# A new load order, six buffers for transposed weight blocks, one DRAM round trip removed, and zero matmuls ahead of the first rows

## The chip, the cores and the metric

The kernel runs on one core of a Trainium2 chip. The metric is the device time of one execution in microseconds (us): the median of 3 runs of the kernel before is 375.06 us (373.87 to 377.57). TensorE (PE in the profile) multiplies matrices into PSUM, its weight loads are listed apart as PEld, ScalarE is ACT, VectorE is DVE, GpSimd is POOL, SyncE is SP. Transfers are issued by SP or POOL and carried by 16 DMA engines that all queues share.

## The reference

The kernel computes a layer and its gradients. Forward, with x of 2048 rows by 448 columns:

```
n  = layernorm(x)                      # over the 448 columns
h  = x + irfft2(rfft2(n) * (w_r + i w_i))
u  = gelu(einsum("bsd,sf->bdf", layernorm(h), w1) + b1)
out= h + transpose(einsum("bdf,fs->bds", u, w2) + b2)
```

Here w1 is 2048 by 1792 and w2 is 1792 by 2048. Backward, from grad_out: the gradients of x, w_r, w_i, w1, b1, w2 and b2. Everything is bfloat16 at the borders. The Fourier transforms are written as products with tables of cosines and sines.

## The kernel before

**Stages on TensorE.** `fft_rows` (L311) multiplies folded, normalized rows of x by a small table, in four groups g of four row tiles h. `fft_cols` (L321 to L343) does the transform over columns and leaves the spectrum `xs`. `cmul` (L362 to L365, VectorE) multiplies it by the weights `w_t`. `ifft_cols` (L377, L378) and `ifft_rows` (L405 to L414, once for each of 16 row tiles) go back. Between them lies a product that needs nothing of this: `dg(j)` (L434), 14 blocks j of 16 matmuls of 448 columns, w2 transposed times grad_out. Its blocks stand in the program after the Fourier work, and the planner that puts the instructions of each engine in a fixed order sets them into the places where TensorE would wait. After them come `gelu_in` (L515, w1 times the normalized h), the second product of the forward pass (L582, w2), the gradient through w1 (L637, w1 transposed), the backward Fourier stages with `gw2` (L656) between them, and the last gradient (L726). An engine executes its instructions strictly in the planned order: one that waits holds up all that stand behind it.

**The first rows.** For each group g, `Norm.stats` (L279, L281, VectorE) takes mean and variance of four row tiles; `Norm.finish` (L289 to L296) computes the reciprocal deviation and lets ScalarE write the normalized rows `xln`; VectorE folds them into `eo` (L303 to L305); TensorE runs 16 matmuls of 128 columns (L311); the results are cast from PSUM into `zt` by ScalarE or VectorE (L194, L196) as the letters in `"avav"` say (a is ScalarE, v is VectorE). `dg(j)` may not start before `fft_rows` of group min(j-1, 3) has been issued; `dg(0)` is free.

**The load queue.** Nearly all loads stand in one chain on SP: `nxt` ties each one behind the one before it (`tc.issue_after(chain[-1].ins)`), so the order in which the lines are traced is the order in which SP issues them. Up to the last chunk of w1 it is:

```
x0, grad_out 0, x1, grad_out 1, w2T0, x2, x3, w2T1, w2T2, w2T3, w2T4 (after dg 0),
df1, hf, w_r, w_i, w2T5, w2T6, w2T7, hi, di0, kinv, ident, xln_d 0..3 (stores),
w2T8, w2T9, w1c0, w2T10, xs_d (store), w2T11, w1c1, w2T12, w2T13, w1c2, w1c3
```

`w2T` j is a block of w2 loaded with a transposing DMA (L175); it lies in the ring `w4` of four buffers, so that the load j+4 waits until `dg(j)` has read its buffer. The ring is used again for `w1T` (transposed w1, L637), `s6` and `s4` (results on their way out). `w1c` are the chunks of w1 (two DMAs each), `df1`, `hf`, `hi`, `di0`, `kinv`, `ident` are tables. Loads outside the chain (`w1T`, `w2c`) are placed by the planner.

**Two scratch tensors in DRAM** matter here. `xln_d` receives the normalized x after the first stage, by four DMAs on SP, and is read back by four DMAs on POOL into `xr` near the end, where the backward pass of the first layernorm needs it (`norm_back`, L605 to L613). `xs_d` receives the spectrum.

**Biases.** b1 and b2 are turned into columns by two small matmuls with the identity (L503), traced after `dg(13)`, and copied out of PSUM by VectorE (L504).

Of the kernel before, what the change touches and what calls it, by code (L numbers as in the profile page):

```python
# [113 lines left out]
def kernel(  # L114
# [32 lines left out]
    def w4(shape, name):  # L147
        return ring.tile(shape, BF16, tag="w4", bufs=4, name=name)

# [94 lines left out]
    for g in range(2):  # L244
        nxt(ld, go_nat[:, 8 * g:8 * g + 8, :],
            grad_out[0].rearrange("(t p) d -> p t d", p=P)[:, 8 * g:8 * g + 8, :])
        if g == 0:
            load_x(1)
    load_w2T()
    load_x(2)  # L250
    load_x(3)
    for j in range(3):
        load_w2T()

    rstd_x = consts.tile([P, NT], F32, name="rstd_x")
    rstd_h = consts.tile([P, NT], F32, name="rstd_h")
    rneg_x = consts.tile([P, NT], F32, name="rneg_x")
    rneg_h = consts.tile([P, NT], F32, name="rneg_h")
    gb1 = consts.tile([P, NFB], F32, name="gb1")
    gb2 = consts.tile([P, NT], F32, name="gb2")  # L260

    xln_d = dram.tile([P, NT, D], BF16, name="xln_d")
    xs_d = dram.tile([P, 2, XW], BF16, name="xs_d")
# [6 lines left out]
    class Norm:  # L270
        def __init__(self, src, dst, rstd, rneg, eps_col, scale, back, nm):
            self.src, self.dst, self.rstd, self.eps_col, self.scale, self.nm = src, dst, rstd, eps_col, scale, nm
            self.rneg, self.back = rneg, back
# [11 lines left out]
        def finish(self, g):  # L285
            mv = self.mv[:, :].rearrange("p (i c) -> p i c", c=2)
            r = self.rstd[:, 4 * g:4 * g + 4]
            sq = col(4, f"sq_{self.nm}")
            ac.activation(out=sq[:], in_=mv[:, :, 1], func=ACT.Sqrt, bias=self.eps_col[:], scale=self.scale)  # L289
            ve.reciprocal(out=r, in_=sq[:])  # L290
            ve.tensor_scalar(out=self.rneg[:, 4 * g:4 * g + 4], in0=r, scalar1=self.back, scalar2=None, op0=ALU.mult)
            nb = col(4, f"nb_{self.nm}")
            ve.scalar_tensor_tensor(out=nb[:], in0=mv[:, :, 0], scalar=-1.0, in1=r, op0=ALU.mult, op1=ALU.mult)
            for i in range(4):
                h = 4 * g + i
                ac.activation(out=self.dst[:, h, :], in_=self.src[:, h, :], func=ACT.Identity,  # L296
                              scale=self.rstd[:, h:h + 1], bias=nb[:, i:i + 1])

# [71 lines left out]

    def ifft_cols(ys, ab):
        def half(r):
            pt = ps_sp([P, 2, 2, P])
            lo = 1 if r <= 8 else 0
            for c in range(2):
                k = r * DF + 97 * c
                pe.matmul(pt[:, c, :, :], lhsT=ys[:, 0, k:k + P], rhs=hi[:, lo:lo + 2, r, :], start=True, stop=False)  # L377
                pe.matmul(pt[:, c, :, :], lhsT=ys[:, 1, k:k + P], rhs=hi[:, 1 - lo:3 - lo, r, :],  # L378
                          start=False, stop=True)
            return pt  # L380

# [36 lines left out]
    xln = slot(1, [P, NT, D], "xln")  # L418
    nx = Norm(x, xln, rstd_x, rneg_x, eps_x, 1.0, -1.0 / D, "x")
    zt = slot(2, [P, 4, NR, P], "zt")  # L420
    folded = []
    for g in range(4):
        for i in range(4):
            nx.stats(4 * g + i)
        folded.append(fft_rows(xln, zt, g, "avav" if g else "aava"))

# [11 lines left out]
    dg(0)  # L438
    df1 = table([P, 6 * DF], "df1", "df")
    hf = consts.tile([P, 3, NR, P], BF16, name="hf")  # L440
    nxt(ld, hf[:, 0:2], hnd["hf"].ap())
    w_t = slot(4, [P, 2, XW], "w_t")
    load_w(w_t, nxt)
    for j in range(1, 4):
        dg(j)
    hi = consts.tile([P, 3, NR, P], BF16, name="hi")
# [48 lines left out]
    b1col = consts.tile([P, NFB], F32, name="b1col")  # L495
    b2col = consts.tile([P, NT], F32, name="b2col")
    b1r = consts.tile([NFB, P], BF16, name="b1r")
    ld(b1r[:], B_b1.rearrange("(j p) -> j p", p=P), po)
    b2r = consts.tile([NT, P], BF16, name="b2r")
    ld(b2r[:], B_b2.rearrange("(t p) -> t p", p=P), po)  # L500
    for src, dst, n in ((b1r, b1col, NFB), (b2r, b2col, NT)):
        pb = ps_mm([P, n], BF16)
        pe.transpose(pb[:], src[:], ident[0:n, 0:n])  # L503
        ve.tensor_copy(out=dst[:], in_=pb[:])  # L504

# [115 lines left out]
    for h in range(NT):  # L621
# [143 lines left out]
```

## Time and profile before

| what | value |
|---|---|
| median of 3 runs | 375.06 us |
| the profiled execution, whole | 375.83 us |
| its span, first to last instruction | 374.1 us |
| first matmul | 11.77 us into the span |
| TensorE busy | 350.1 us, 94% |
| VectorE, ScalarE busy | 236.5 us, 217.7 us |
| moved by DMA | 86.48 MB, 231 GB/s on the mean |
| busy share of the DMA engines, 0 to 94 us | 8 tenths in the first slice, then 9 or more in nine slices |

All times in the text are counted from the start of the span unless said otherwise; 1.7 us of the profiled execution lie around the span. "Landing" of a DMA is the time at which its last data are there. The chain of waits is followed back from the last instruction; a number in square brackets at the end of a line of the timeline is how long the engine sat idle before the group, and who ended it.

### The profile page before, as it was taken

Reading aid. Unit: us, or ns where it says so; the run is one execution under the profiler, and the core shown is the slowest. Engines: PE = TensorE matmul, PEld = TensorE weight load, DVE = VectorE, ACT = ScalarE, POOL = GpSimd, SP = SyncE. Lnnn points to the kernel's source line nnn. Section 1 sums busy time; section 2 is a strip of 40 time slices with the busy share of each in tenths; the row PEclk is TensorE's granted clock in tenths of the full one; section 3 lists DMA queues with packets and bytes.
Section 4 is the critical chain, followed back from the end, with each engine's and each line's share of the span. In section 5 each row is a group of like instructions: output and inputs, shape, how many; then the busy total and the mean of one; then the engine's idle time right before and its main releaser. Section 6 shows DMA issues by size and latency. Waiting matters only on the chain.

```text
span 374.1 us, 5776 instructions
## 1 busy us (share of the span) xinstructions
PE 350.1 (94%) x2115; PEld 201.4 (54%) x2115; DVE 236.5 (63%) x557; ACT 217.7 (58%) x415; POOL 61.5 (16%) x107
## 2 busy tenths in 40 slices
PE   0798999987999999999999999999999999999996
PEld 0455667654664555555555555566655555655553
DVE  4863679872772999911257778648996576699000
ACT  3585545344558999490012243776665666777664
POOL 1000000000113111422240000100012522355211
PEclk9999999998999999999999999999999999999999
DMA  8999999999799999994998877591694353956633
GB/s 286 271 241 294 259 262 268 301 305 238 207 269 308 342 361 338 401 275 114 172 202 173 174 152 240 115 217 64 170 231 182 149 187 150 330 216 249 237 149 147
DMA packets 132524, 86.48 MB, mean 231 GB/s; under 512 B 91952, under 2 KB 123824, under 8 KB 131984
## 3 DMA queue, kind: packets, MB, share of 16 engines
q1 hardware_dynamic: 124304, 55.78, 60.7%
q0 software_dynamic: 8048, 30.31, 21.8%
q8 instruction: 16, 0.26, 0.3%
q14 instruction: 12, 0.10, 0.1%
q10 hardware_dynamic: 144, 0.03, 0.0%
HBM read 32.81 MB, written 30.76 MB: 170 GB/s over the span
## 4 chain that ended last, share of the span: by engine, by line
PE 67%; DVE 18%; ACT 7%; DMA 4%; issue 2%; SPq 1%; ACTq 0%; DVEq 0%
PE ps_mm L726 12%; PE ps_mm L656 10%; PE ps_mm L434 8%; PE ps_sp L582 7%; PE ps_mm L515 6%; PE ps_sp L515 5%; PE ps_mm L582 4%; DVE junk L610 3%; DVE junk L612 3%; ACT v L605 3%; DMA w2T<-in_B_w_dram 3%; DVE t_r L362 2%; DVE gg L349 2%; DVE t_i L363 2%; PE ps_sp L321 2%
## 5 line engine op out<-in xcount | busy, mean ns | idle before, releaser
L194 ACT CAST s<-ps_mm 128x512 bf16<-128x512 f32 (+1 forms) x107 | 57.6, 557 | 25.6 <-PE ps_mm L656 11.0
L656 PE MATMUL ps_mm<-goT,g_t 128*128 128x512 bf16 x224 | 55.2, 379 | 1.6 <-ACT s L194 1.5
L434 PE MATMUL ps_mm<-go_nat,w2T 128*128 128x448 bf16 x224 | 52.3, 367 | 3.7 <-DMA w2T<-in_B_w_dram 3.7
L726 PE MATMUL ps_mm<-du_t,hlnT 128*128 128x512 bf16 (+1 forms) x256 | 49.6, 352 | 0.0
L637 PE MATMUL ps_mm<-du,w1T 128*128 128x449 bf16 x224 | 43.4, 353 | 0.0
L605 ACT ACTIVATE v<-ps_mm,nm,rstd_h 128x448 f32<-128x448 f32 x16 | 11.6, 725 | 53.4 <-DVE nm L603 53.4
L726 PEld LDWEIGHTS <-hlnT 128*128 128x128 bf16 x256 | 25.0, 98 | 22.2
L582 PE MATMUL ps_sp<-gT,w2c 128*128 128x448 bf16 x140 | 35.6, 352 | 0.0
L172 POOL DMA_DIRECT2D out_dram<-s x29 | 15.7, 541 | 113.9 <-ACT s L194 87.8
L434 PEld LDWEIGHTS <-w2T 128*128 128x128 bf16 x224 | 22.4, 101 | 20.0 <-DMA w2T<-in_B_w_dram 4.6
L582 PEld LDWEIGHTS <-w2c 128*128 128x128 bf16 x224 | 21.9, 98 | 20.5
L637 PEld LDWEIGHTS <-w1T 128*128 128x128 bf16 x224 | 21.7, 97 | 20.7
L515 PEld LDWEIGHTS <-w1c 128*128 128x128 bf16 x224 | 21.8, 98 | 20.5 <-issue 1.8
L656 PEld LDWEIGHTS <-g_t 128*128 128x128 bf16 x224 | 21.6, 97 | 20.6 <-issue 1.4
L349 DVE TENSOR_TENSOR gg<-ps_sp,gi 128x450 bf16<-128x450 f32 x28 | 16.2, 619 | 17.0 <-ACT gi L346 17.0
L194 ACT CAST eo<-ps_sp 128x450 bf16<-128x450 f32 x32 | 17.2, 538 | 14.8 <-PE ps_sp L407 14.5
L582 PE MATMUL ps_mm<-gT,w2c 128*128 128x448 bf16 x84 | 25.0, 352 | 0.0
L515 PE MATMUL ps_mm<-hln,w1c 128*128 128x448 bf16 x112 | 24.3, 352 | 0.7 <-DVE b1col L504 0.5
L515 PE MATMUL ps_sp<-hln,w1c 128*128 128x448 bf16 x112 | 23.1, 352 | 0.0
L587 DVE SCALAR_TENSOR_TENSOR h<-ps_sp,b2col,hr 128x448 bf16<-128x448 f32 x10 | 6.3, 678 | 25.1 <-PE ps_sp L582 25.1
L311 PE MATMUL ps_sp<-kf,eo 128*128 128x128 bf16 x128 | 9.3, 231 | 13.4 <-DVE eo L305 13.4
L610 DVE CUSTOM_DVE_ANT_0 junk<-ps_sp,xr,rneg_x 128x448 bf16<-128x448 f32 x16 | 10.9, 682 | 16.3 <-ACT v L607 16.3
(146 smaller groups left out, 626.5 us busy)
## 6 DMA issues: line engine op xcount, KB each, us to landing
w1c<-in_B_w_dram SPq DMA_DIRECT2D x7, 1024.0 KB, 8.3
w2c<-in_B_w_dram SPq DMA_DIRECT2D x8, 896.0 KB, 10.5
out_dram<-s POOLq DMA_DIRECT2D x14, 512.0 KB, 3.1
out_dram<-s POOLq DMA_DIRECT2D x15, 448.0 KB, 3.1
xs_d<-xs SPq DMA_DIRECT2D x1, 1800.0 KB, 7.9
xs_b<-xs_d SPq DMA_DIRECT2D x1, 1800.0 KB, 8.1
x<-in_A_x_dram SPq DMA_DIRECT2D x4, 448.0 KB, 4.2
go_nat<-in_grad_out_dram SPq DMA_DIRECT2D x2, 896.0 KB, 6.9
```

The costliest lines, as they stand in the source:

```text
L172: return (eng or po).dma_start(out=out, in_=in_)
L194: ac.copy(out=out, in_=in_)
L349: ve.tensor_tensor(out=gg[:], in0=pr[:], in1=gi[:], op=op)
L434: pe.matmul(pg[:], lhsT=w2T[j][:, t, :], rhs=go_nat[:, t, :], start=(t == 0), stop=(t == NT - 1))
L515: pe.matmul(pu[:], lhsT=wc[:, h, o:o + P], rhs=hln[:, h, :], start=(h == 0), stop=(h == NT - 1))
L582: pe.matmul(p2[i][:], lhsT=w2c[t0 // 4][:, j, i * P:(i + 1) * P], rhs=gT[:, j, :], start=(j == 0), stop=(j == NFB - 1))
L605: ac.activation(out=v[:], in_=ps[:, 0:D], func=ACT.Identity, scale=rstd_c, bias=nm1[:])
L610: ve.tensor_tensor_reduce(out=junk[:], in0=ps[:, 0:D], in1=xhat, scale=rneg_c, scalar=0.0, op0=ALU.mult, op1=ALU.add, accum_out=nm2[:])
L612: ve.scalar_tensor_tensor(out=junk[:], in0=xhat, scalar=nm2[:], in1=v[:], op0=ALU.mult, op1=ALU.add)
L637: w1_last = pe.matmul(pd[:], lhsT=w1T[:, j, :], rhs=du[:, j, 0:D + 1], start=(j == 0), stop=(j == NFB - 1))
L656: mm = pe.matmul(pw[:], lhsT=g_t[:, c, j * P:(j + 1) * P], rhs=goT[:, c, 512 * n:512 * n + 512], start=(c == 0), stop=(c == 3))
L726: pe.matmul(pw[:, 0:wdt], lhsT=hlnT[:, c, h * P:(h + 1) * P], rhs=du_t[:, c, 512 * n:512 * n + wdt], start=(c == 0), stop=(c == 3))
```

## The change

It has seven parts.

1. `idle`, a tile of zeros of 128 by 512, is written by VectorE, and 34 matmuls of it stand first in TensorE's order. Nobody reads their result.
2. The ring `w4` has six buffers in place of four.
3. The chain of loads has another order: `w2T1` before x2 and x3; `w2T5` behind `df1` and `hf` and ahead of w_r and w_i; `w2T` 9 and 10 after the tables; all the other `w2T` blocks before w1c0 and `xs_d`. The result is

```
x0, grad_out 0, x1, grad_out 1, w2T0, w2T1, x2, x3, w2T2, w2T3, w2T4, df1, hf, w2T5,
w2T6 (after dg 0), w_r, w_i, w2T7, w2T8, hi, di0, kinv, ident, w2T9, w2T10,
w2T11, w2T12, w2T13, w1c0, xs_d (store), w1c1, w1c2, w1c3
```

4. `xln_d` is gone. Near the end `xr` is loaded from x itself, and VectorE normalizes it again in place, 16 instructions, with the kept reciprocal deviation and the now kept product `nbias`.
5. Groups 1 to 3 of the first rows cast `"aava"` in place of `"avav"`: one cast each goes from VectorE to ScalarE.
6. The two bias matmuls are tied behind the last matmul of `ifft_cols` and traced before `ifft_rows`.
7. The loads `w2c` and `w1T` are tied behind the last load of the chain, w1c3.

```diff
     def w4(shape, name):
-        return ring.tile(shape, BF16, tag="w4", bufs=4, name=name)
+        return ring.tile(shape, BF16, tag="w4", bufs=6, name=name)
...
+    idle = consts.tile([P, 512], BF16, name="idle")
+    ve.memset(idle[:], 0.0)
+    pz0 = ps_mm([P, 512])
+    for i in range(34):
+        pe.matmul(pz0[:], lhsT=idle[:, 0:P], rhs=idle[:], start=True, stop=True)
...
-    load_w2T()
+    for j in range(2):
+        load_w2T()
     load_x(2)
     load_x(3)
     for j in range(3):
         load_w2T()
+    df1 = table([P, 6 * DF], "df1", "df")
+    hf = consts.tile([P, 3, NR, P], BF16, name="hf")
+    nxt(ld, hf[:, 0:2], hnd["hf"].ap())
+    load_w2T()
...
-        folded.append(fft_rows(xln, zt, g, "avav" if g else "aava"))
+        folded.append(fft_rows(xln, zt, g, "aava"))
...
     dg(0)
-    df1 = table([P, 6 * DF], "df1", "df")
-    hf = consts.tile([P, 3, NR, P], BF16, name="hf")
-    nxt(ld, hf[:, 0:2], hnd["hf"].ap())
     w_t = slot(4, [P, 2, XW], "w_t")
     load_w(w_t, nxt)
-    for j in range(1, 4):
-        dg(j)
+    dg(1)
+    dg(2)
...
-    for g in range(4):
-        nxt(ld, xln_d[:, 4 * g:4 * g + 4, :], xln[:, 4 * g:4 * g + 4, :])
+    for j in range(3, 5):
+        dg(j)
...
-    for j in range(4, NFB):
+    for j in range(5, NFB):
         dg(j)
-        if j == 6:
-            nxt(ld, xs_d[:], xs[:])
-        if j in (5, 7, 13):
+        if j == 7:
+            load_w1c(nxt)
+            nxt(ld, xs_d[:], xs[:])
+            load_w1c(nxt)
+        if j == 13:
             load_w1c(nxt)
...
         pb = ps_mm([P, n], BF16)
-        pe.transpose(pb[:], src[:], ident[0:n, 0:n])
+        with tc.issue_after(cols_last.ins):
+            pe.transpose(pb[:], src[:], ident[0:n, 0:n])
...
-            ld(t[:, :, k:k + 256],
-               B_w2.rearrange("(j p) s -> p j s", p=P)[:, :, 512 * c + k:512 * c + k + 256])
+            with tc.issue_after(chain[-1].ins):
+                ld(t[:, :, k:k + 256],
+                   B_w2.rearrange("(j p) s -> p j s", p=P)[:, :, 512 * c + k:512 * c + k + 256])
...
-        w1T_last = ld_t(w1T[:], w1Tv[h])
+        with tc.issue_after(chain[-1].ins):
+            w1T_last = ld_t(w1T[:], w1Tv[h])
...
-            ld(xr[:], xln_d[:, h:h + 4, :], po)
+            ld(xr[:], rows(A_x[0])[:, h:h + 4, :], po)
+
+            for i in range(4):
+                ve.tensor_scalar(out=xr[:, i, :], in0=xr[:, i, :], scalar1=rstd_x[:, h + i:h + i + 1],
+                                 scalar2=nbias_x[:, h + i:h + i + 1], op0=ALU.mult, op1=ALU.add)
```

More of the change, by code (lines that the diff above doesn't have):

```diff
@@ L258 @@
     rneg_h = consts.tile([P, NT], F32, name="rneg_h")
+    nbias_x = consts.tile([P, NT], F32, name="nbias_x")
+    nbias_h = consts.tile([P, NT], F32, name="nbias_h")
     gb1 = consts.tile([P, NFB], F32, name="gb1")
     gb2 = consts.tile([P, NT], F32, name="gb2")
-    xln_d = dram.tile([P, NT, D], BF16, name="xln_d")
     xs_d = dram.tile([P, 2, XW], BF16, name="xs_d")
@@ L270, with __init__ @@
     class Norm:
-        def __init__(self, src, dst, rstd, rneg, eps_col, scale, back, nm):
+        def __init__(self, src, dst, rstd, rneg, nbias, eps_col, scale, back, nm):
+            self.nbias = nbias
             self.src, self.dst, self.rstd, self.eps_col, self.scale, self.nm = src, dst, rstd, eps_col, scale, nm
@@ L291, in finish @@
             ve.tensor_scalar(out=self.rneg[:, 4 * g:4 * g + 4], in0=r, scalar1=self.back, scalar2=None, op0=ALU.mult)
-            nb = col(4, f"nb_{self.nm}")
-            ve.scalar_tensor_tensor(out=nb[:], in0=mv[:, :, 0], scalar=-1.0, in1=r, op0=ALU.mult, op1=ALU.mult)
+            ve.scalar_tensor_tensor(out=self.nbias[:, 4 * g:4 * g + 4], in0=mv[:, :, 0], scalar=-1.0, in1=r, op0=ALU.mult, op1=ALU.mult)
             for i in range(4):
@@ L296, in finish @@
                 ac.activation(out=self.dst[:, h, :], in_=self.src[:, h, :], func=ACT.Identity,
-                              scale=self.rstd[:, h:h + 1], bias=nb[:, i:i + 1])
+                              scale=self.rstd[:, h:h + 1], bias=self.nbias[:, h:h + 1])
     def fft_rows(src, zt, g, on, behind=None):
@@ L371, in ifft_cols @@
     def ifft_cols(ys, ab):
+        lasts = []
         def half(r):
@@ L377, in half @@
                 pe.matmul(pt[:, c, :, :], lhsT=ys[:, 0, k:k + P], rhs=hi[:, lo:lo + 2, r, :], start=True, stop=False)
-                pe.matmul(pt[:, c, :, :], lhsT=ys[:, 1, k:k + P], rhs=hi[:, 1 - lo:3 - lo, r, :],
-                          start=False, stop=True)
+                last = pe.matmul(pt[:, c, :, :], lhsT=ys[:, 1, k:k + P], rhs=hi[:, 1 - lo:3 - lo, r, :],
+                                 start=False, stop=True)
+            lasts.append(last)
             return pt
@@ L398, in ifft_cols @@
                 "p c h k l -> p k c h l"), in0=view(p0), in1=view(t1), op=ALU.subtract)
+        return lasts[-1]
     def ifft_rows(ab, itab, h):
@@ L418 @@
     xln = slot(1, [P, NT, D], "xln")
-    nx = Norm(x, xln, rstd_x, rneg_x, eps_x, 1.0, -1.0 / D, "x")
+    nx = Norm(x, xln, rstd_x, rneg_x, nbias_x, eps_x, 1.0, -1.0 / D, "x")
     zt = slot(2, [P, 4, NR, P], "zt")
@@ L464 @@
     ab = slot(5, [P, 2, 2, NT, NR, 8], "ab")
-    ifft_cols(w_t, ab)
+    cols_last = ifft_cols(w_t, ab)
+    b1col = consts.tile([P, NFB], F32, name="b1col")
+    b2col = consts.tile([P, NT], F32, name="b2col")
+    b1r = consts.tile([NFB, P], BF16, name="b1r")
+    ld(b1r[:], B_b1.rearrange("(j p) -> j p", p=P), po)
+    b2r = consts.tile([NT, P], BF16, name="b2r")
+    ld(b2r[:], B_b2.rearrange("(t p) -> t p", p=P), po)
+    for src, dst, n in ((b1r, b1col, NFB), (b2r, b2col, NT)):
+        pb = ps_mm([P, n], BF16)
+        with tc.issue_after(cols_last.ins):
+            pe.transpose(pb[:], src[:], ident[0:n, 0:n])
+        ve.tensor_copy(out=dst[:], in_=pb[:])
     hn = x
     hln = slot(1, [P, NT, D], "hln")
-    nh = Norm(hn, hln, rstd_h, rneg_h, eps_h, 1.0 + LN_EPS, -(1.0 + LN_EPS) / D, "h")
+    nh = Norm(hn, hln, rstd_h, rneg_h, nbias_h, eps_h, 1.0 + LN_EPS, -(1.0 + LN_EPS) / D, "h")
     for h in range(NT):
@@ L485, in load_w1c @@
             on(ld, w1c[c][:, :, k:k + 256], w1v[:, :, 512 * c + k:512 * c + k + 256])
-    for j in range(4, NFB):
+    for j in range(5, NFB):
         dg(j)
-        if j == 6:
+        if j == 7:
+            load_w1c(nxt)
             nxt(ld, xs_d[:], xs[:])
-        if j in (5, 7, 13):
             load_w1c(nxt)
[L495 to L502, printed above, removed]
-        pe.transpose(pb[:], src[:], ident[0:n, 0:n])
-        ve.tensor_copy(out=dst[:], in_=pb[:])
+        if j == 13:
+            load_w1c(nxt)
     gT = slot(3, [P, NFB, D], "gT")
```

## The prediction

> **What bounds it now.** I read the shares first, then TensorE's waits, then the timeline at each of them, then SP's queue.
>
> ```profile
> PE 350.1 (94%) x2115; PEld 201.4 (54%) x2115; DVE 236.5 (63%) x557; ACT 217.7 (58%) x415; POOL 61.5 (16%) x107
> ...
> PE ps_sp L311 <- DVE eo L305: 13.4, 3, 11.8
> PE ps_mm L434 <- DMA w2T<-in_B_w_dram: 3.7, 2, 3.0
> PE ps_mm L656 <- ACT s L194: 1.5, 3, 0.7
> PE ps_mm L515 <- DVE b1col L504: 0.5, 1, 0.5
> ```
>
> TensorE is busy 94%. Its waits (total, times, longest) are the first 11.8 us, 1.4 us before group 3 of the first rows, 3.7 us for w2T, 0.5 us for a bias copy, and crumbs. From 118 us on almost nothing is left to win; what is gained must come out of the first 100 us.
>
> ```profile
> 11.77 1.89 PE L311 MATMUL ps_sp<-kf,eo 128*128 128x128 bf16 x16 [11.77 <-DVE eo L305]
> 13.45 6.14 PE L434 MATMUL ps_mm<-go_nat,w2T 128*128 128x448 bf16 x21
> 26.50 3.19 PE L434 MATMUL ps_mm<-go_nat,w2T 128*128 128x448 bf16 x16
> 31.08 1.07 PE L311 MATMUL ps_sp<-kf,eo 128*128 128x128 bf16 x16 [1.39 <-DVE eo L305]
> 75.72 0.36 PE L434 MATMUL ps_mm<-go_nat,w2T 128*128 128x448 bf16 x1 [0.65 <-DMA w2T<-in_B_w_dram]
> 86.14 1.68 PE L434 MATMUL ps_mm<-go_nat,w2T 128*128 128x448 bf16 x4 [3.01 <-DMA w2T<-in_B_w_dram]
> ```
>
> Not all loss is waiting. 16 matmuls of 448 take 3.19 us at 26.50, their starts 0.19 us apart; right after 11.77 TensorE is slower, as the weight loads show, which follow the matmuls:
>
> ```profile
> 14.19 0.15 PEld L434 LDWEIGHTS <-w2T 128*128 128x128 bf16 x1 [0.22 <-issue]
> 14.57 0.15 PEld L434 LDWEIGHTS <-w2T 128*128 128x128 bf16 x1 [0.22 <-issue]
> ```
>
> They are 0.37 us apart until 17.53: half pace for 5.76 us, a loss of 2.9 us. The table by stretches, here the one around the 3.01 us wait, has the granted clock in the third column from the end:
>
> ```profile
> 83.13:89.12 5.99, 2.98 (x14) 1.78 (x14) 1.67 (x7) 3.25 (x5) 0.78 (x1) 0.72 1.02 216
> ```
>
> It is 0.72 there, and 1.00 in the first stretches, where the pace alone tells. The pieces after 86.14 take 2.98 us; at the later pace they are 4 x 0.19 + 8 x 0.098 = 1.54. So that wait costs 3.01 + 1.44.
>
> Why is w2T late at 86 us? SP's queue:
>
> ```profile
> 57.07 2.39 SPq L169 DMA_DIRECT2D w1c<-in_B_w_dram  x2
> 59.51 6.46 SPq L175 DMA_TRANSPOSE w2T<-in_B_w_dram  x1
> 66.06 0.53 SPq L169 DMA_DIRECT2D xs_d<-xs  x1
> 66.69 7.00 SPq L175 DMA_TRANSPOSE w2T<-in_B_w_dram  x1
> 73.79 2.55 SPq L169 DMA_DIRECT2D w1c<-in_B_w_dram  x2
> 76.39 10.35 SPq L175 DMA_TRANSPOSE w2T<-in_B_w_dram  x2
> ```
>
> Between the blocks stand 4 x 1024 KB of w1, first used at 98.5, and 1800 KB of `xs_d`. The DMA engines are full here, so the order decides.
>
> **C, w2T before w1 and xs_d: -5.1 us.** The two waits and the slow restart are 0.65 + 3.01 + 1.44 = 5.1. How late is the last block in the new order? (Landings are from the trace's DMA issues.) ident lands at 49.58 now, behind eight blocks; it will stand behind nine. One block costs 2.0 us (w2T6 and 7 land at 40.57 and 42.57) to 3.4 us (w2T1 and 2, 17.28 and 20.68); the four `xln_d` stores that shared those microseconds are gone. Say ident at 50 to 52. Five blocks follow, 9 to 13, at 2.0 to 3.4: the last lands at 60 to 69. With six buffers block j waits for dg(j-6); dg(7) ends at 57.18 now, so this holds w2T13 no longer. dg(12) is at 83, dg(13) at 91: 14 us to spare. What becomes late next is w1c0 and w1c1: 4 x 1024 + 1800 KB took 57.07 to 82.75 with three blocks between; behind 60 to 69 without them they land by 80 to 90, w1c1 being used from about 125. w1c2 needs dg(13) done, as now. So nothing takes the place of this wait; I take it whole. Ends: 0, if the planner puts other fillers there, and 5.1.
>
> **A, clock and first rows: -1.5 us.** The zeros start at about 1.3 us (after DVE's memsets, 0.82 to 0.94, and that of `idle`, which I estimate at 0.1 to 0.7 from the 0.06 us memset of one column and the 0.69 us tensor_scalar of 2048 columns). At half pace 512 columns take 0.37 x 512/448 = 0.43 us, then 0.22. With 5.76 us of half pace as measured, 13 cost 5.6, the other 21 cost 4.6: done at 11.5, just before 11.77. Then 2.9 us of half pace are gone. But the rest isn't TensorE's: x2 and x3 move behind w2T1, which SP issues at 10.25 in place of them; they land 2.0 to 3.4 us later than 14.20 and 15.31. Group 0 shows the path from landing to `eo`: 4.29 to 11.72, 7.4 us. So group 2 is ready at about 23.6 to 25.0 (25.55 now). Group 3 follows through ScalarE, whose xln of groups 2 and 3 start 5.5 us apart (21.54, 27.01), 0.8 of it waiting for TensorE; `"aava"` adds a cast of 0.59 there (VectorE loses 0.69). So 5.3 us: 28.9 to 30.3 in place of 31.03. By TensorE alone group 3 could start at 11.77 + 3 x 0.9 + 4 x 3.05 = 26.7. I take the middle of ScalarE's, 1.5 us sooner. Behind them waits the table hf, 31.01 now and as many bytes ahead of it after; its first use is at 34.30, so no more than 3.3 us can be gained here. Ends: +1 (x3 late by 3.4 and nothing gained back) and -3.3.
>
> The Trainium skill, "TensorE: Matmul & The Clock Gate", Part 1, says that TensorE starts at half clock and is let go after about 3.4 us of activity in a free-running window, and that it falls back only after an idle window of that length. By its figure the zeros would end at 10.4, an estimate, and the sum would not change. This trace differs on the second half: 3.01 us without a matmul were enough to slow it. The page also puts the whole ramp below 1% of a typical span, which speaks for a small A.
>
> **B, biases: -0.5 us.** The 0.54 us at 98.5 goes: b1col is made 27 us sooner. On VectorE the copy now stands among the `ab` additions, where it is busy 5.00 of 5.00 us (60 to 70), and two of three `ps_mm` buffers are held till then; dg needs one. Ends -0.5 and +0.5.
>
> **D, what is added.** w_r and w_i now come behind w2T5 and w2T6: wi lands at 31.0 + 2 x (2.0 to 3.4) + 4.45 = 39.5 to 42.3 (35.46 now); VectorE's first t_i is at 43.72, 42.2 when A is won. It is in VectorE's order ahead of `gg`, which TensorE waits for: 0 to 0.7, I take 0.2. `xr`: 16 tensor_scalar, nearest row
>
> ```profile
> L521 DVE TENSOR_SCALAR zz<-zz 128x448 bf16<-128x448 bf16 x5 | 1.4, 279 | 0.1
> ```
>
> 4.5 us on VectorE, which in 280 to 330 is busy 32.4 of 50 us and has nothing after 346 while TensorE runs to 370. In 260 to 280 it is full, and if the first 8 stand there `ab` comes 2.2 us later; gw2 covers this if planned so. 0 to 2.2, I take 0.3. Its load is the same 448 KB on POOL. The stores of `xln_d`, 1.8 MB and SP from 42.26 to 46.32, end nothing on TensorE's chain: 0, counted under C. More buffers for s6 and s4: 1.5 us of waits there are for ScalarE, 0. w2c tied behind w1c3: issued behind it now (118.35 after 109.67), 0.
>
> **Sum.** 375.83 - 5.1 - 1.5 - 0.5 + 0.5 = 369.2 for the profiled execution; the median stands 0.8 lower, so **368.4**.
>
> **Rivals.**
> 1. *x2 and x3 late eat the start.* A is 0 or +1: 369.9 to 370.9. For it: ScalarE's chain through group 3 is the present limit. Against: VectorE and ScalarE idle 4.3 and 2.1 us there. 0.16.
> 2. *Fillers run out.* dg is done sooner, and `ifft_rows`, which now has 4 matmuls (0.76 us) of it per row tile, runs bare. VectorE needs 0.63 + 0.63 + 0.18 per tile, 1.4, TensorE 0.8: 0.6 us for each bare tile, some 6 before hln feeds gelu_in: +3.6, 372.0. Against: TensorE's total before 98 us is the same, and it has been full since 31 us. 0.11.
> 3. *Slower: six w1T ahead of w2c0.* Now four w1T lie between the w1 chunks (86.85 to 107); tied behind w1c3, and with two more buffers, up to six can be put before w2c0. SP reaches them at about 102 (w1c3 at 109.67 now, less 7.5). At 3.3 us each on SP they end at 122, w2c0 lands at 127 and 136 (6.1 and 14.6 after 118.35 now), needed at 139. From about 5 us each on (one took 7.03 at 100.63) w2c0 is 7 us late and all is lost; at 7 us, 19 us late: 387. 0.07.
> 4. *The zeros do nothing*, since the clock slows again before the rows: A shrinks to about -0.5, 369.4; they overrun only if half pace lasts on: 1.3 + 34 x 0.43 = 15.9, 4.1 us late, 374.0 without A. 0.06.
> My forecast, 365 to 370.5, has 0.60.
>
> **Range.** All good ends (A 3.3, B 0.5, C 5.1, D 0) give 366.2 by the median; if hf doesn't hold A back either (2.9 + 1.39), 365.2, and with the waits of 0.30 and 0.17 at 110 to 114 gone too, 364.7. Above, rivals 1, 2 and most of 4 are in: 373.5. A change under 1% (3.75 us) can't be told from none in runs that spread over 3.7 us. Faster by more, below 371.3: 0.60 + 0.16 + 0.05 of rival 4, less 0.05 for what of these lies above: 0.76. Slower: rival 3, and 0.01 for an overrun with more behind it: 0.08. Same: rival 2 and those 0.05: 0.16.
>
> **What would show it.** No w2T among TensorE's waits; weight loads 0.19 apart from the first dg on; group 3 at 28 to 30; last w2T landed before 70; PE's last matmul 6 to 8 us sooner; 16 tensor_scalar near 0.28. Wrong if a wait appears at 32 to 45 (hf, w_t), at `ifft_rows`, or for w2c0 near 139.

## The result, and the profile after

The changed kernel takes **392.9 us** (median of 6 runs, 391.16 to 397.69) where the kernel before, beside it on the same chip, takes 375.64 (6 runs, 373.87 to 378.70): a ratio of 1.0444, with a 95% interval of 1.0392 to 1.0497. Medians here are of all runs, while ratios and their intervals leave out the runs that were more than 1.5% slower than the fastest of the same kernel. The change makes the kernel 17 us slower; the forecast was 7 us faster and its range ended at 373.5. The profiled execution took 391.31 us, its span 389.5.

From the page of the changed kernel: busy time by engine, and TensorE and the DMA engines in 40 slices of 9.7 us (a digit is tenths, 9 is 90% or more):

```profile
PE 358.2 (92%) x2134; PEld 204.0 (52%) x2149; DVE 242.0 (62%) x571; ACT 220.0 (56%) x418; POOL 61.4 (16%) x107
...
PE   8777557899999999999999999999996999999996
...
DMA  8999990048999999999999993192490653866544
```

PE's busy time now holds 9.7 us of zeros, ahead of the first rows. New are the digits 55 of PE (TensorE half empty from 39 to 58 us) and the two zeros of the DMA engines (standing from 58 to 78). TensorE's waits in the changed kernel (total, times, longest):

```profile
PE ps_sp L333 <- DVE gg L361: 10.0, 7, 1.6
PE ps_sp L323 <- DVE eo L317: 4.1, 4, 1.7
PE ps_mm L675 <- DVE s L196: 2.6, 2, 2.1
PE ps_sp L323 <- DVE rstd_x L303: 2.4, 1, 2.4
PE ps_sp L391 <- ACT t L408: 1.7, 6, 0.3
```

The 3.7 us for w2T are gone, as forecast. In their place TensorE waits 10.0 us for `gg` within `fft_cols` (0.3 before), 1.7 for `t` within `ifft_cols`, 4.1 and 2.4 for the first rows, and 2.1 in one piece for a cast `s` near the end. The timeline of TensorE in the changed kernel shows where:

```profile
11.94 1.07 PE L323 MATMUL ps_sp<-kf,eo 128*128 128x128 bf16 x16 [0.91 <-DVE eo L317]
...
26.89 1.07 PE L323 MATMUL ps_sp<-kf,eo 128*128 128x128 bf16 x16 [2.44 <-DVE rstd_x L303]
...
33.62 3.19 PE L450 MATMUL ps_mm<-go_nat,w2T 128*128 128x448 bf16 x16
...
45.24 0.35 PE L333 MATMUL ps_sp<-gg,hf 128*128 128x450 bf16 x1 [1.28 <-DVE gg L361]
...
74.78 0.18 PE L490 MATMUL ps_mm<-ident,b1r 14*128 14x14 bf16 x1
74.82 0.16 PE L490 MATMUL ps_mm<-ident,b2r 16*128 16x16 bf16 x1
74.91 2.44 PE L450 MATMUL ps_mm<-go_nat,w2T 128*128 128x448 bf16 x12
```

(`...` marks lines left out.) The fifth dg block runs at 33.62; the next matmul of dg stands at 74.91, right behind the two bias matmuls (`b1r`, `b2r`). For 38 us, through all of `fft_cols` and `ifft_cols`, there is no dg work to fill TensorE's waits: 80 matmuls of dg are done before `ifft_cols` ends, 157 in the kernel before, and TensorE's gaps from the first matmul of `fft_cols` to the last of `ifft_cols` add up to 13.5 us (0.4 before). SP's queue in the changed kernel shows the echo:

```profile
47.41 43.60 SPq L175 DMA_TRANSPOSE w2T<-in_B_w_dram  x5
91.11 5.52 SPq L169 DMA_DIRECT2D w1c<-in_B_w_dram  x2
```

Five blocks take 43.60 us to issue, since block 11 needs the buffer that dg(5) gives back; it goes out at 78.34, and w1 only at 91.11. The last block lands at 94.33; the prediction had it before 70.

Where the 15.7 us between the two last matmuls (370.7 and 386.4 us) arise can be read from the ends of the stages. The table has the profiled executions of both kernels and of the main experiments, in us from the start of the span:

| | before | after | bias back | + x first | + xln_d back | + untied | scaled on GpSimd |
|---|---|---|---|---|---|---|---|
| first rows, group 3 starts | 31.1 | 32.7 | 33.5 | 30.8 | 29.9 | 31.2 | 30.4 |
| `ifft_cols` ends | 70.9 | 74.8 | 75.7 | 72.9 | 74.6 | 73.4 | 72.5 |
| dg ends | 97.8 | 116.3 | 92.5 | 89.8 | 91.5 | 90.2 | 89.4 |
| `gelu_in` ends | 146.9 | 158.7 | 146.3 | 143.6 | 145.2 | 144.0 | 143.2 |
| product with w1T ends | 234.0 | 246.6 | 236.0 | 237.7 | 240.5 | 231.1 | 230.2 |
| last matmul | 370.7 | 386.4 | 377.3 | 378.7 | 377.1 | 367.8 | 366.9 |

11.8 us are lost up to `gelu_in`, 0.8 from there to w1T, 3.1 behind it. The third to sixth columns of times undo one part of the change after the other (the runs e1_bias_back, e4_x_first, f1_xln_back and f2_untied); the last is one of the experiments' own versions (h3_pool_scale). A column is one execution and not a median: the one for "bias back" took 382.19 us, the fastest of four with a median of 386.06, and the one for "x first" 383.72, with a median of 382.19. So the last row does not order these two as their medians do.

### The profile page after: what moved, and what is told of

Same layout as the page of the kernel before. It is cut to its first block, busy times and chain, and to the rows that moved or that the text cites. A ratio compares the mean times of both kernels' runs of the same rounds, so it can differ in the third digit from the quotient of the medians.

```text
span 389.5 us, 5825 instructions
## 1 busy us (share of the span) xinstructions
PE 358.2 (92%) x2134; PEld 204.0 (52%) x2149; DVE 242.0 (62%) x571; ACT 220.0 (56%) x418; POOL 61.4 (16%) x107
## 4 chain that ended last, share of the span: by engine, by line
PE 44%; DVE 20%; issue 15%; ACT 10%; DMA 4%; SPq 3%; POOL 2%; ACTq 0%; POOLq 0%; DVEq 0%
PE ps_mm L749 12%; PE ps_mm L675 6%; PE ps_mm L450 6%; PE ps_mm L532 4%; PE ps_sp L532 3%; DVE junk L630 3%; DVE junk L628 3%; ACT v L623 3%; SPq L175 2%; DVE gg L361 2%; PE ps_sp L391 2%; DVE t_r L374 2%; PE ps_sp L333 1%; ACT hln L308 1%; PE ps_sp L392 1%
## 5 line engine op out<-in xcount | busy, mean ns | idle before, releaser
L675 PE MATMUL ps_mm<-goT,g_t 128*128 128x512 bf16 x214 | 53.3, 379 | 4.8 <-DVE s L196 2.6
L450 PE MATMUL ps_mm<-go_nat,w2T 128*128 128x448 bf16 x224 | 46.1, 352 | 0.0
L172 POOL DMA_DIRECT2D out_dram<-s x29 | 15.7, 541 | 94.3 <-ACT s L194 73.4
L450 PEld LDWEIGHTS <-w2T 128*128 128x128 bf16 x224 | 21.6, 98 | 16.4
L612 ACT ACTIVATE junk<-go_r 128x448 bf16<-128x448 bf16 x16 | 9.2, 576 | 25.0 <-DMA go_r<-in_grad_out_dram 24.6
L532 PE MATMUL ps_mm<-hln,w1c 128*128 128x448 bf16 x112 | 22.3, 352 | 0.0
L532 PE MATMUL ps_sp<-hln,w1c 128*128 128x448 bf16 x112 | 22.3, 352 | 0.0
L333 PE MATMUL ps_sp<-gg,hf 128*128 128x450 bf16 x32 | 11.3, 354 | 11.5 <-DVE gg L361 10.0
```

Of the source, the lines that this page charges most:

```text
L172: return (eng or po).dma_start(out=out, in_=in_)
L333: pe.matmul(px[:, :], lhsT=hf[:, 0, r, :], rhs=gg[:, :], start=True, stop=False)
L450: pe.matmul(pg[:], lhsT=w2T[j][:, t, :], rhs=go_nat[:, t, :], start=(t == 0), stop=(t == NT - 1))
L532: pe.matmul(pu[:], lhsT=wc[:, h, o:o + P], rhs=hln[:, h, :], start=(h == 0), stop=(h == NT - 1))
L675: mm = pe.matmul(pw[:], lhsT=g_t[:, c, j * P:(j + 1) * P], rhs=goT[:, c, 512 * n:512 * n + 512], start=(c == 0), stop=(c == 3))
```

## The experiments

All kernels here compute the whole result. "Before" differs a little from chip to chip (375.6 to 378.2 us), so ratios are what is compared.

### Part 6, the biases: three runs

The theory: the planner hands out the buffers of a PSUM ring in the order in which the program is traced. The bias matmuls take theirs from the ring of three that dg uses, they are traced ahead of dg(5), and they are tied behind `ifft_cols`; so dg(5) and all behind it can't be placed before `ifft_cols` has ended. First the part undone in the changed kernel:

```diff
-        with tc.issue_after(cols_last.ins):
-            pe.transpose(pb[:], src[:], ident[0:n, 0:n])
+        pe.transpose(pb[:], src[:], ident[0:n, 0:n])
```

The lines are also traced behind dg(13) again.

> The changed kernel, with part 6 alone undone: the two bias matmuls stand behind dg(13) again and are tied to nothing. Theory R (ring): the bias matmuls take their PSUM buffers from ps_mm, the ring of three that dg uses too; buffers of a ring are given out in the order in which the lines are traced, so dg(5) to dg(13), traced behind the biases, can't get one before the last matmul of ifft_cols. R expects dg back between 36 and 75 us, TensorE's 14 us of waits there gone, and about 372 us (375.6 less the 5.1 of the w2T waits, plus 1.6 because group 3 of the first rows comes at 32.7 in place of 31.1). Theory Q (queue): the new order of the loads makes the planner put dg late. Q expects 390 to 393 us as now.

Measured: 386.06 us (4 runs), ratio 1.0252 (1.0187 to 1.0316), 6.8 us less than the changed kernel by the medians. What theory R said of the place came true: 169 matmuls of dg stand before the end of `ifft_cols`, the gaps there are 0.2 us, and `gelu_in` ends 12.4 us sooner. Its 372 us did not: the kernel is still slower than the kernel before. And only 9.1 of the 12.4 us reach the last matmul. Behind `gelu_in`, TensorE waits 2.5 us for `h` (0.7 in the changed kernel), and after a wait for a cast `s` its granted clock was 0.50 for 3.4 us (1.00 at that place in the changed kernel), which costs another 1.7: together about what is given back. Both come up again below. The part alone, put into the kernel before:

> The kernel before, with part 6 alone: the bias matmuls tied behind ifft_cols and traced ahead of ifft_rows. R: dg(4) to dg(13) all come after ifft_cols. 73 of their matmuls that now stand ahead of it, 13.8 us, move behind it, while the Fourier stages get little shorter; less the w2T waits of 5.1 us, which vanish because the loads have time: 384 to 391 us. Q: no change, 375 to 376 us.

Measured: 410.64 us, ratio 1.0902 (1.0841 to 1.0963): alone it costs 34 us, twice the whole change. Exactly four blocks of dg (64 matmuls) are done before `ifft_cols` ends, as R said; its 384 to 391 us took the waits for w2T as gone, and they grew. TensorE's waits in it:

```profile
PE ps_mm L438 <- DMA w2T<-in_B_w_dram: 17.6, 4, 9.3
PE ps_sp L311 <- DVE eo L305: 13.7, 3, 12.2
PE ps_sp L321 <- DVE gg L349: 10.0, 7, 1.6
```

The same 10.0 us for `gg`, and 17.6 for w2T: there blocks 10 to 13 stand between w1's chunks and `xs_d`, and when dg starts late these loads start late one after the other (blocks 10, 11 and 12 land at 105.2, 119.0 and 132.1). In the changed kernel, with its order of loads, no such wait is there; that the order softens part 6 is my reading, no run tests it alone. Third, the tie and the place kept, only the ring changed:

```diff
-        pb = ps_mm([P, n], BF16)
+        pb = ps_sp([P, n], BF16)
```

> The changed kernel with the tie and the place of the bias matmuls kept, but their PSUM buffers taken from the other ring, ps_sp, whose later users come after ifft_cols anyway. R: 371 to 373 us, dg between 36 and 75 us. If the tie or the place itself did the harm (theory T), or Q: 390 to 393 us.

Measured: 385.39 us (2 runs), ratio 1.0234 (1.0188 to 1.028), 168 matmuls of dg before the end of `ifft_cols`: as good as undoing the part, though as far from R's 371 to 373 us as the first run was from its 372. Neither the tie nor VectorE's copy costs the time; it is the ring.

### Part 3, x2 and x3 behind w2T1

```diff
-    for j in range(2):
-        load_w2T()
+    load_w2T()
     load_x(2)
     load_x(3)
-    for j in range(3):
+    for j in range(4):
         load_w2T()
```

> As e1, and x2 and x3 ahead of w2T1 again. The trace of the changed kernel has x2 landing at 17.17 (14.20 before), VectorE waiting 3.68 us for it with the fold of group 1 planned behind it, and group 3 at 32.71. If that is the cause, group 3 comes at 28.5 to 30, and the time is 2 to 4 us below e1: 368 to 370. If ScalarE's chain with one cast more is the cause, less than 1 us below e1.

Measured, on top of the first experiment: 382.19 us, ratio 1.0127 (1.0066 to 1.0188), 3.9 us less, within the 2 to 4 us that were expected of it. Group 3 starts at 30.75 in place of 33.49. In the changed kernel x2 lands at 17.17 (14.20 before) and this is VectorE's timeline there:

```profile
17.19 0.63 DVE L292 BATCH_NORM_STATS2 bs_x<-x 128x6 f32<-128x448 bf16 x1 [3.68 <-DMA x<-in_A_x_dram]
17.74 0.61 DVE L315 TENSOR_TENSOR eo<-xln 128x892 bf16<-128x892 bf16 x1
...
25.58 0.63 DVE L315 TENSOR_TENSOR eo<-xln 128x892 bf16<-128x892 bf16 x1 [1.50 <-ACT xln L308]
```

The statistics of x2 stand ahead of the fold of group 1 in VectorE's order, so VectorE sits idle for 3.68 us with that fold behind it; from the landing of x2 to the end of group 2's fold it takes 9.7 us.

### Part 4, x scaled again in place of `xln_d`

Alone in the kernel before (the edit is the next diff turned round, with the kept `nbias_x`):

> Edit: the kernel before with the change's fourth part alone (no stores of x's normal form; xr is x, loaded again and scaled by 16 tensor_scalar). Theory N as above: the 16 operations cost 2.5 to 4 us in the stretch before the last product, the 3.5 us of stores that go save nothing that ends late: 378 to 380 against 376. Rival of the prediction's term D (0.3 us): 375.5 to 376.9. A gain of 1 us or more would say that the stores delayed the transposed blocks of w2 behind them.

Measured: 380.44 us, ratio 1.0138 (1.0071 to 1.0204). TensorE's waits in it, the second and third lines:

```profile
PE ps_mm L435 <- DMA w2T<-in_B_w_dram: 6.0, 2, 5.0
PE ps_mm L655 <- DVE s L196: 2.1, 1, 2.1
```

The wait for `s` is there, and the stretch from the start of the backward `ifft_rows` to the last product grows from 36.1 to 38.2 us. The other 2.5 us lie in the front, where w2T is waited for 6.0 us and not 3.7: fewer stores, yet block 12 landed at 88.29 in place of 86.10, and the granted clock after that wait was 0.50 for 6.8 us in place of 3.4. Why the block came later stays open. The mechanism near the end, from VectorE in the first experiment (bias back):

```profile
284.10 2.53 DVE L693 TENSOR_SCALAR xr<-xr,rstd_x,nbias_x 128x448 bf16<-128x448 bf16 x8
...
289.56 0.70 DVE L693 TENSOR_SCALAR xr<-xr,rstd_x,nbias_x 128x448 bf16<-128x448 bf16 x2
290.17 1.28 DVE L196 CAST s<-ps_mm 128x512 bf16<-128x512 f32 x2
```

and from TensorE in the same run:

```profile
290.91 4.87 PE L674 MATMUL ps_mm<-goT,g_t 128*128 128x512 bf16 x14 [2.09 <-DVE s L196]
```

Twelve of the 16 operations stand ahead of the casts that give TensorE its PSUM buffers back. One takes 0.39 us by its row; eight in a row take 2.53 us. Undone in the changed kernel, on top of the two edits above:

```diff
+    xln_d = dram.tile([P, NT, D], BF16, name="xln_d")
...
+    for g in range(4):
+        nxt(ld, xln_d[:, 4 * g:4 * g + 4, :], xln[:, 4 * g:4 * g + 4, :])
...
-            ld(xr[:], rows(A_x[0])[:, h:h + 4, :], po)
-
-            for i in range(4):
-                ve.tensor_scalar(out=xr[:, i, :], in0=xr[:, i, :], scalar1=rstd_x[:, h + i:h + i + 1],
-                                 scalar2=nbias_x[:, h + i:h + i + 1], op0=ALU.mult, op1=ALU.add)
+            ld(xr[:], xln_d[:, h:h + 4, :], po)
```

> Edit: e4_x_first with the change's fourth part undone (the four stores of x's normal form are back behind ident, xr is loaded from them, no tensor_scalar and no bias of x in it). Theory N (the renormalising scaled on VectorE is what the stretch from 283 to 300 us loses: 16 operations of 389 ns planned ahead of the casts s, so that TensorE waits 2.09 us for s and then runs at half pace): that wait is gone and the stage from the end of the second block product to the gw1 product is about 3 us shorter, time about 378 to 379.5 against 382.2 of e4_x_first. Rival (N has its price hidden, the stage is late for what comes before it): within 1 us of e4_x_first, and the wait for s is there without the scaling. The stage with w1T stays as late as in e4_x_first under both (start to end about 52 us, 45 in the kernel before).

Measured: 381.0 us, ratio 1.014 (1.0061 to 1.022): by the ratio no different from 1.0127. The wait for `s` is gone and that stretch is 36.1 us long in place of 39.9. What was won there had been lost before: `gelu_in` ends 1.7 us later, the product with w1T another 1.1. At 61.9 us TensorE waits 2.80 us for w2T, a wait that the profiled execution without the stores does not have; for the product with w1T it waits 5.9 us for `h` and not 4.9. So the theory held for its place and missed for the time; the next part was still in the way.

### Part 7, the ties behind w1c3

Undone on top of all that:

```diff
-            with tc.issue_after(chain[-1].ins):
+            if True:
                 ld(t[:, :, k:k + 256],
...
-        with tc.issue_after(chain[-1].ins):
-            w1T_last = ld_t(w1T[:], w1Tv[h])
+        w1T_last = ld_t(w1T[:], w1Tv[h])
```

> Edit: f1_xln_back with the change's seventh part undone as well (the loads of w2's second form and of w1's transposed blocks carry no tie). Theory Q (in the tied order the transposing loads of w1 and the two tables stand between the loads of w2's second form in SyncE's queue, g_t and goT are sent later and land beside the stores of h, TensorE then waits 2.5 to 4.9 us for h): the stage with w1T is 5 to 7 us shorter, time 371.5 to 374, ahead of the kernel before. Rival (the stage is long for the lack of something else, the six blocks' buffers for w1T among it, which let more loads of w1 go early): the stage stays within 2 us of f1_xln_back's and so does the time.

Measured: **373.76 us** (10 runs), ratio 0.9939 (0.9901 to 0.9976), 7.2 us less than with the ties and faster than the kernel before. SP's queue with the ties (`xln_d` back):

```profile
75.42 33.11 SPq L169 DMA_DIRECT2D w1c<-in_B_w_dram  x5
108.58 11.37 SPq L175 DMA_TRANSPOSE w1T<-in_B_w_dram  x2
121.53 15.91 SPq L169 DMA_DIRECT2D w2c<-in_B_w_dram  x4
137.49 11.34 SPq L175 DMA_TRANSPOSE w1T<-in_B_w_dram  x2
...
169.34 4.64 SPq L169 DMA_DIRECT2D go_r<-in_grad_out_dram  x2
```

and without them:

```profile
73.86 10.38 SPq L175 DMA_TRANSPOSE w1T<-in_B_w_dram  x2
84.34 3.06 SPq L169 DMA_DIRECT2D w1c<-in_B_w_dram  x2
87.49 14.10 SPq L175 DMA_TRANSPOSE w1T<-in_B_w_dram  x2
...
126.48 29.44 SPq L169 DMA_DIRECT2D w2c<-in_B_w_dram  x8
156.02 3.51 SPq L169 DMA_DIRECT2D go_r<-in_grad_out_dram  x2
```

w1c2 waits for its buffer to 91 us, w1c3 to 108. Untied, w1T fills that time; tied, the queue stands, and all six w1T come later, between the loads of w2c. The row of the table by stretches (DMA share and GB/s are the last two columns), with the ties and without:

```profile
100.00:110.00 10.00, 7.66 (x54) 5.16 (x54) 7.01 (x19) 5.03 (x9) 1.30 (x2) 1.00 0.55 176
```

```profile
100.00:110.00 10.00, 7.93 (x52) 5.04 (x52) 6.76 (x19) 5.17 (x10) 1.85 (x3) 1.00 1.17 278
```

All that follows in the queue is 13 us later with the ties. How does that reach TensorE? GpSimd's queue in the run with the ties:

```profile
158.60 0.76 POOL L169 DMA_DIRECT2D hr<-hn_d  x1
191.14 0.54 POOL L172 DMA_DIRECT2D out_dram<-gb2b  x1 [31.77 <-ACT gb2b L615]
191.67 3.74 POOL L172 DMA_DIRECT2D out_dram<-h  x7
```

and VectorE and TensorE in it:

```profile
195.48 1.27 DVE L606 SCALAR_TENSOR_TENSOR h<-ps_mm,b2col,hr 128x448 bf16<-128x448 f32 x2 [7.07 <-DMA out_dram<-h]
196.22 2.03 PE L657 MATMUL ps_mm<-du,w1T 128*128 128x449 bf16 x5 [5.87 <-DVE h L606]
```

grad_out's second load lands at 181.76 (169.34 untied), ScalarE's 16 sums over it end at 190.6, and GpSimd has stood for 31.77 us at the small store of these sums with twelve stores of h behind it; VectorE has no buffer for h, TensorE none for its result. After the wait the granted clock was 0.50 from 193.7 to 200.5, so that the products with w1T take 53.0 us and not the 44.9 of the untied version. Read so, moving that one store should have been enough:

```diff
-    st(out_7.rearrange("(q h) -> q h", h=NT), gb2b[:])
+    with tc.issue_after(h2_last.ins):
+        st(out_7.rearrange("(q h) -> q h", h=NT), gb2b[:])
```

> Edit: f1_xln_back (381.0 us, with the tie of the seventh part) and one more tie: the small store of the sums gb2b is put behind the last store of h in GpSimd's queue; SyncE's order of the loads stays as it is. Theory H (the tied order brings grad_out's second load late, ScalarE's 16 sums over it end late, and GpSimd's queue stands at the store of gb2b with the stores of h behind it, so that the buffers of h, VectorE and TensorE wait, 5.9 us): that wait is gone, 374.5 to 376. Rival (the stores of h are slow because g_t, goT and they share the DMA engines; or w1T itself is late behind goT): the stores go earlier but TensorE waits then for w1T, 378 to 381.

Measured: 383.0 us (4 runs), ratio 1.0165 (1.0003 to 1.0326). Nothing is won: theory H fell, and the rival's second half came. The stores of h go early and the wait for h is gone, but:

```profile
PE ps_mm L657 <- DMA w1T<-in_B_w_dram: 5.1, 1, 5.1
```

The queue is late as a whole, and the next thing out of it that TensorE needs is late by nearly as much; the clock falls again (0.50 from 208.6 to 215.4), and the products with w1T take 52.7 us. The chain over the store was real, and only the nearer of two.

Last, the ties alone undone in the changed kernel:

> Edit: the changed kernel (392.9 us) with the seventh part alone undone. Theory H with part 6 in place: the front is 12 us late, so the loads have caught up with the products when h is reached, and only 0.7 us of wait for h are there to be won: 391 to 393. If the seventh part costs 7 us whatever stands before it: 385 to 387.

Measured: 397.69 us (2 runs), ratio 1.0564 (1.0361 to 1.0767). Neither expectation: the ties *help* the changed kernel, by 5 us in the medians. The intervals of the two ratios overlap, but the profiled executions agree with it: without the ties `gelu_in` ends at 166.2 in place of 158.7 and the last matmul at 392.5 in place of 386.4. With dg late, w1 is late, and four untied w1T go in front of its last chunks, which are issued at 134.8 in place of 116.3; TensorE's waits have a new line:

```profile
PE ps_mm L532 <- DMA w1c<-in_B_w_dram: 4.9, 1, 4.9
```

So part 7 guards w1 against the delay that part 6 makes, and costs 7 us once parts 6, 4 and the place of x2 and x3 are undone. The tie on w2c and that on w1T were only undone together.

### Parts 1, 2 and 5: the zeros, the buffers, the casts

The zeros alone in the kernel before, then taken out of the untied version:

```diff
+    idle = consts.tile([P, 512], BF16, name="idle")
+    ve.memset(idle[:], 0.0)
+    pz0 = ps_mm([P, 512])
+    for i in range(34):
+        pe.matmul(pz0[:], lhsT=idle[:, 0:P], rhs=idle[:], start=True, stop=True)
```

> Edit: the kernel before with the 34 multiplications of zeros alone, on the same operands as in the changed kernel. The prediction's term A, the part of it that is the clock's: the first group of rows at full pace instead of 1.89 us and the dg block behind it too, 1 to 1.5 us, so 374 to 375.5 against 376 if what stands behind it is bound by TensorE. Rival (TensorE waits for x2 and x3 anyway, the time won is waited for again before the second and third group of rows): within 0.5 us of the kernel before.

Measured: 377.51 us (12 runs), ratio 1.0042 (1.0011 to 1.0072), slightly slower. Group 3 starts at 29.91 (31.08), `ifft_cols` ends 0.7 sooner, and then TensorE waits 6.7 us for w2T in place of 3.7. Where the loads set the pace, a start 1.2 us sooner is waited for again: 1.4 us at 17.5 already, and 4.2 in place of 3.0 at 87, where block 12 lands at 87.09 in place of 86.10, for a reason that I can't name. After that last wait the granted clock was 0.50 for 6.8 us (85.2 to 92.0), in the kernel before for 3.4 (85.8 to 89.2), and dg ends 1.9 us later than there.

> Edit: f2_untied without the zeros. If the zeros are worth 1 to 1.5 us there: 374.5 to 375.5 against 373.8 of f2_untied. If x2 and x3 set the start anyway: 373.3 to 374.2. If f2_untied owes its whole gain on the kernel before (2.4 us) to the zeros: 376.

Measured: 372.45 us (10 runs), ratio 0.9923 (0.9886 to 0.9959), against 0.9939 with them. The zeros buy nothing here either. With them TensorE waits 1.98 us for w2T1 at 18 us and then runs at a granted clock of 0.50 for 3.4 us; without them that wait is not there, and group 3 starts at 31.41 in place of 31.21.

Four buffers, and the casts as before, each in the untied version:

```diff
-        return ring.tile(shape, BF16, tag="w4", bufs=6, name=name)
+        return ring.tile(shape, BF16, tag="w4", bufs=4, name=name)
```

> Edit: f2_untied with four buffers for the transposed blocks of w2 and w1, not six. The prediction's term C (the blocks of w2 early, ahead of w1's chunks, end the 3.7 us for which TensorE waited for them between 74 and 90 us) needs room for the blocks: with four buffers the blocks traced ahead of w1's chunks make the queue stand until dg frees a buffer, w1's chunks land late, and the time is 2 to 5 us above f2_untied, 376 to 379. If the order alone does it: within 1 us of f2_untied.

Measured: 373.74 us (10 runs), ratio 0.9955 (0.9912 to 0.9997), the same as with six. The last w2T lands at 72.50 and not 69.85, still more than 10 us before it is needed. It is the order that ends the waits of 0.65 and 3.01 us at 76 and 86 us; the two more buffers do nothing here. Not every wait for w2T is gone: with the zeros and with x2 and x3 first there is one of 1.5 to 2.4 us at 18 us, and in the profiled executions of f1_xln_back, f3_avav, k1_gb2_late and this run one of 0.8 to 2.8 us at 60 to 62.

```diff
-        folded.append(fft_rows(xln, zt, g, "aava"))
+        folded.append(fft_rows(xln, zt, g, "avav" if g else "aava"))
```

> Edit: f2_untied with the change's fifth part undone too (the last three groups of rows are copied out by ScalarE and VectorE in turn as before, no longer three by ScalarE for each one by VectorE). I have no strong reason for a difference: VectorE has the fold of each group and the statistics, so 'aava' should take load from it, and rows3 comes 0.5 us or so later without it. Time within 1.5 us of f2_untied; above 2 us in either way would mean that the copies bound the start.

Measured: 373.92 us (10 runs), ratio 0.9957 (0.9914 to 1.0), no difference that these runs can tell.

### A version that beats both

Part 4 in again, its 16 operations moved to the idle engine:

```diff
-                ve.tensor_scalar(out=xr[:, i, :], in0=xr[:, i, :], scalar1=rstd_x[:, h + i:h + i + 1],
+                po.tensor_scalar(out=xr[:, i, :], in0=xr[:, i, :], scalar1=rstd_x[:, h + i:h + i + 1],
```

> Edit: f2_untied with the change's fourth part in it again (no stores of x's normal form), but the 16 operations that scale x once more given to GpSimd, which is busy 16% of the span, in place of VectorE. Theory N (what part 4 costs is VectorE's place ahead of the casts s): no wait for s, the stores' 1 to 2 us in the front are won, 371.5 to 373.5. Rival (GpSimd is slow at it, at several us for each operation, and the last product waits for xr; or it slows VectorE beside it): 375 and more.

Measured: **371.79 us** (4 runs, 371.44 to 371.95), ratio 0.9881 (0.983 to 0.9931). It keeps the new load order (with x2 and x3 in their old place), the zeros, the six buffers, the casts of part 5 and the freed stores, and drops parts 6 and 7. GpSimd's row for the operation:

```profile
L691 POOL TENSOR_SCALAR xr<-xr,rstd_x,nbias_x x16: 705/707/1154, 273.0 to 302.0; 128x448 bf16<-128x448 bf16 x16
```

0.71 us each at the median, nearly twice VectorE's 0.39, but TensorE's wait for a cast `s` by VectorE is gone, and the stretch from the backward `ifft_rows` to the last product is 36.1 us long, as in the kernel before. Without the zeros:

> Edit: h3_pool_scale without the zeros. The zeros have bought nothing in two places (377.5 with them against 375.6 without in the kernel before, 373.8 against 372.5 in f2_untied): 370.5 to 371.8 against 371.8. If the zeros do help once the start isn't held by other things: 372.5 to 373.

Measured: 372.69 us (4 runs), ratio 0.9899 (0.9799 to 0.9999). By the time, this lies in the band for "the zeros do help", 0.9 us above the version with them; but the two ran on different chips, and the ratios, 0.9881 and 0.9899, differ by far less than their intervals are wide. By the medians the zeros are 0.9 us better here, 1.9 us worse in the kernel before and 1.3 us worse in the untied version: the three pairs show no gain that holds.

## Why the prediction was wrong

**Step B failed, and it is the largest error.** It priced the bias matmuls at -0.5, with ends of 0.5 either way, on the words "two of three `ps_mm` buffers are held till then; dg needs one". That takes a ring for a pool. The buffers are handed out in traced order, as the run with the other ring bears out, so dg(5) had to come after the biases in that ring, and those were tied behind `ifft_cols`. The step counted how long VectorE holds the buffers and didn't ask from when TensorE is kept from them. In the table this is the 12.4 us up to `gelu_in`. No rival had this mechanism, and the range could not hold it. B alone does not explain the sign: without part 6 the kernel is still 2.5% slower than the kernel before, and the errors in A and D, below, make up the rest.

**Step C was right about the wait, and mis-sized.** "No w2T among TensorE's waits" is what the profile shows, and with the biases free dg ends at 92.5 in place of 97.8. But "nothing takes the place of this wait; I take it whole" failed. From the start of group 3 to the end of `gelu_in` the kernel before takes 115.8 us, the run with the biases back 112.8, and so do the untied version and the one that scales on GpSimd: 3.0 us won, not 5.1. What takes the place is a wait in `ifft_rows`, 0.3 us in the kernel before and 2.3 in each of these three; in the run with the biases back:

```profile
PE ps_sp L427 <- ACT eo L194: 2.3, 4, 0.7
```

With dg done sooner nothing is left to fill four of its row tiles. That is rival 2 ("fillers run out", held at 0.11), at the place it named and at 2.3 us for its 3.6; in the changed kernel part 6 hid it. C's reason "with six buffers ... this holds w2T13 no longer" was not needed, four do as well; and in the changed kernel it was not true, since block 11 waited for the late dg(5).

**Step A had the wrong sign.** Forecast 1.5 us sooner at group 3; measured 1.6 later. The zeros did what was computed for them: half pace until 5.53 us, done at 11.03 (forecast 11.5), the first rows in 1.07 us and not 1.89. What failed is the time from landing to `eo` in the loads' part, "Group 0 shows the path from landing to `eo`: 4.29 to 11.72, 7.4 us". It takes 9.7 for group 2, because VectorE works on group 1's fold and casts in between, and those had waited for x2 themselves; with x2 and x3 back in their place group 3 starts 2.7 us sooner. It is rival 1 (held at 0.16), a little dearer than its +1.

**Step D was mis-sized twice, and its zero for the ties was wrong.** The 0.279 us for a `tensor_scalar` came from a row with an immediate operand; with two columns as operands it took 0.389. And the case it named itself, operations standing ahead, "0 to 2.2, I take 0.3", is the one that came, with twelve of them in place of the first eight: 2.1 us of wait and up to 3.8 with what follows it. "w2c tied behind w1c3: issued behind it now (118.35 after 109.67), 0" looked at the order of w2c alone. What the tie moves is w1T, and so the whole queue, by 13 us: 5 us won in the changed kernel, 7.2 lost once part 6 is out of the way. Rival 3 saw a danger in w1T standing ahead of w2c0; that didn't come, as in the changed kernel w2c0 goes out at 126.8 and the first w1T at 143.5.

The account, by the ratios: undone one after the other, part 6 gives 0.019, the place of x2 and x3 0.0125, part 4 nothing that can be told (-0.001), part 7 0.020, together 0.05 or 19 us. The parts don't add: part 6 alone in the kernel before costs 34 us. The version so left (untied) is 2.7 us (0.6%) faster than the kernel before, and the profiled executions have these 2.9 us at the end of `gelu_in` already, which is step C's 3.0. Run by run the gain is less sure, as the clock goes into it: on that chip the runs of the kernel before whose granted clock was 0.998 or more over the whole execution took 372.8 to 374.4 us (5 of 19), those of the untied version 372.0 to 375.5 (7 of 10), with a median of 373.6 for both. How much of the 2.7 us is the clock stays open. For the version that scales on GpSimd the same comparison, 371.4 to 372.0 (4 of 4) against 372.7 to 374.8 (11 of 27), leaves about 2 us.

## What to carry to other kernels

A tie that delays one small instruction also delays whoever comes after it in the same ring of buffers: before tying an instruction, look up which ring it draws from and which work that now fills gaps is traced behind it. Where a transfer queue is full, an order that lets it stand while it waits for one buffer is paid for at the far end, by whatever comes out of the queue next; if moving one waiter away doesn't help, look at the whole queue. Work put on a busy engine should be weighed by what is planned behind it there; here an engine that was idle 84% of the time did it at about half the speed and kept nobody waiting.

## What the hardware showed that I had not expected

A short wait can slow TensorE's clock, or not. After 2.09 us without a matmul (the run with the biases back) the stretch that followed had a granted clock of 0.66 (third column from the end), 14 matmuls of 512 columns in 4.87 us:

```profile
291.00:296.00 5.00, 5.00 (x18) 2.09 (x18) 2.64 (x6) 2.19 (x4) 2.15 (x4) 0.66 0.72 274
```

In the changed kernel, after 2.08 us at the same place, it was 1.00 and the 14 took 3.18:

```profile
301.20:306.20 5.00, 4.91 (x27) 2.71 (x28) 3.41 (x9) 2.73 (x5) 2.16 (x4) 1.00 0.68 264
```

The Trainium skill, "TensorE: Matmul & The Clock Gate", Part 1, has the clock fall back after an idle window of about 3.4 us that runs freely. A free-running window fits that the same wait has two outcomes; its length does not fit, as 2.09 us without a matmul were enough here. Nor does the length of the wait decide alone: in the untied version 1.98 us at 18 us were followed by a granted clock of 0.50 for 3.4 us, in the run with `xln_d` back 2.80 us at 62 us by a clock of 1.00. Where the clock fell in mid-run, it stayed at 0.50 for 3.4 or 6.8 us, in the run with part 6 alone also for 10.2: once, twice or three times 3.41. So a wait of about 2 us cost between nothing and 1.7 us more than its length, and I can't tell beforehand which. Part of the spread between executions of one kernel goes with it: the kernel before took 372.7 to 374.8 us where the granted clock over the whole run was 0.998 or more, and 375.4 to 378.9 where it was 0.995 or less (27 runs on one chip). Multiplying zeros lifts the clock as other data does: the weight loads of the zeros are 0.43 us apart up to 5.53 us and 0.22 from 5.91 on.
